# A fused attention and ELU layer on one core: a new written-out order, Strassen for two more groups, DMA transposes for two more blocks

## The chip, the core and the metric

The kernel runs on one NeuronCore of a Trainium2 chip. The metric is the device time of one launch in microseconds (us). TensorE is called PE here, VectorE DVE, ScalarE ACT, GpSimd POOL and SyncE SP. Each has its own instruction stream and runs it in order; they meet at semaphores, and DMA transfers are issued from the SP, ACT and POOL queues.

## What is computed

Decayed linear attention in blocks of 64 rows (4 batches, 8 heads, 768 rows, head size 64), then a dense layer of width 2048 with an ELU and a dense layer back to 512:

```python
for b in range(nb):                       # nb = 12 blocks of 64 rows
    intra = einsum('bhic,bhjc->bhij', qb, kb) * Dmask
    intra = einsum('bhij,bhjd->bhid', intra, vb)
    inter = einsum('bhid,bhde->bhie', qb * lam_pow, kv_state)
    out[:, :, sl] = intra + inter
    kv_state = lam_block * kv_state + einsum('bhsd,bhse->bhde', kb * rev_pow, vb)
x = out.transpose(0, 2, 1, 3).reshape(3072, 512)
h = x @ w_in                              # 512 -> 2048
g = where(h > 0, h, exp(min(h, 0)) - 1)
return g @ w_out                          # 2048 -> 512
```

## The kernel before

The work is cut into 24 steps `s`; a step is one block of 64 rows of two batches, so 128 rows of `x` (even steps belong to batches 0 and 1, odd steps to 2 and 3). What the title of the change calls a block is a step here. Two steps make a group of 256 rows, 12 groups in all. All products are in fp16.

**Attention of a step.** `load` brings `kn`, `qn`, `vn` in with casting DMAs on POOL's queue, in two halves of 64 partitions with rows of 64 numbers; the queries of steps 0 to 5 come as rows of eight (`eights`, one transfer with 2 KB rows), and step 0's keys and queries come uncast on SP's and ACT's queues into `kraw0`, `qraw0`. `visit(so, us, ss, sx)` issues PE work for up to four steps at once: `mm_S` scores of `ss` (into psum tile `Z`), `mm_U` the state update of `us`, `mm_I` and `mm_O` the output of `so`, and the transposes of `sx` (`mm_T`, or for early steps the 128-wide form at lines 398 and 403). Beside it stand, by letter of the order: `C` (`att_C`) copies transposes out of psum, `P` multiplies scores with the mask, `N` adds the new state, `X` (`att_X`) copies the output into `xt`, `V` (`decay_v`) forms `vd` = `vn` times the decay, which `mm_U` reads, `Q` (`decay_q`) forms `qs` and `D` (`decay_s`) forms `sd`. From step `NT` = 10 on the transposes come from `dma_T`, two DMA transposes on SP's queue into `TD`, with two buffers.

**Dense layers of a group.** `mm1_h` (H, line 428) makes 512 columns of `h` in psum tile `psH` (two buffers), 8 such units a group. `mm1_e` or `elu` apply exp and relu on ACT (lines 438, 440, 472, 474), and DVE combines them (`g`, lines 445 and 475). For groups 0, 1 and 2 (steps 0 to 5) the second layer is plain: `mm2` (M, line 495), four pieces of 4 products of 512 columns a step, and `mm2_o` (Z) stores. From group 3 on it is one level of Strassen: `g_sum` (s, line 533) and `w_sum` (B, line 521) form sums on DVE, `part` (p, line 551) runs 7 pieces of 8 products of 256 columns a group, `keep`, `add` and `c2` move and add the parts (lines 581, 585, 589), `store` writes.

**The order.** `tc.manual_schedule()` keeps each engine's stream as the program issues it. Up to step 8 the order is the string `start`, one word per call (`A...2` is a visit that transposes step 2, `V2` is `decay_v(2)`); `later_loads` (word R) and the lines before it fix POOL's load order. From group 3 on, a loop over groups and units interleaves the units with visits, parts and sums. POOL runs `decay_q` and `decay_s` of late steps between its load issues. Each transfer from POOL uses one of eight completion semaphores in turn, so an issue waits for the landing of the eighth transfer before it.

```python
    load("v", 0)
    load_step(1)
    load_wi(0)
    load_step(2)
    load_wi(1)
```

Of the kernel before, what the change touches and what calls it, by code (L numbers as in the profile page):

```python
# [16 lines left out]
def kernel(  # L17
# [41 lines left out]

    NB = 12  # L60

    NT = 10

    NQ = 6
    kn, qn, vn = {}, {}, {}

    def eights(b, c):

        return q[b : b + 2, :, c * L : (c + 1) * L, :].rearrange("r h (p g) d -> (r h) p (g d)", g=8)

    def load(which, s):
        b, c = where(s)
        src, keep, tag = {"k": (k, kn, "kn"), "q": (q, qn, "qn"), "v": (v, vn, "vn")}[which]
        keep[s] = inp.tile([128, H, D], FP16, tag=tag, bufs=NB, name=f"{tag}{s}")
        if which == "q" and s < NQ:
            nc.gpsimd.dma_start(out=keep[s][:].rearrange("p h d -> p (h d)"), in_=eights(b, c))
            return
        for r in range(2):
            nc.gpsimd.dma_start(  # L79
                out=keep[s][half(r)],  # L80
                in_=src[b + r, :, c * L : (c + 1) * L, :].rearrange("h p d -> p h d"),
            )

    def load_step(s):
        load("k", s)
        load("q", s)
        load("v", s)
# [9 lines left out]
    def load_wi(i, halves=range(2)):  # L97

        for c in halves:
            ins = nc.gpsimd.dma_start(  # L100
                out=wi[i][half(c)],
                in_=moe_w_in[c * DM // 2 : (c + 1) * DM // 2, i * WB : (i + 1) * WB].rearrange(
                    "(g p) f -> p g f", p=64
                ),
            )
            if (i, c) == (2, 1):

                ins.wait_op(crossed, 1, "sem-ge")

    def load_wo(i):  # L110
        nc.gpsimd.dma_start(
            out=wo[i][:],
            in_=moe_w_out[i * WB : (i + 1) * WB, :].rearrange("(g p) f -> p g f", p=128),
        )

# [5 lines left out]
    for which, src in (("k", k), ("q", q)):  # L121
        raw0[which] = inp.tile([128, H, D], FP32, name=f"{which}raw0")
        if which == "q":
            nc.scalar.dma_start(out=raw0[which][:].rearrange("p h d -> p (h d)"), in_=eights(0, 0))
            continue
        for r in range(2):
            nc.sync.dma_start(
                out=raw0[which][half(r)], in_=src[r, :, 0:L, :].rearrange("h p d -> p h d")
            )
    load("v", 0)  # L130
    load_step(1)
    load_wi(0)
    load_step(2)
    load_wi(1)
    load_step(3)
    load_wi(2, [0])

# [95 lines left out]
    def att_C(s):  # L233
        if s >= NT:
            return
        T = asb.tile([128, 2, NHP, 2, L], FP16, tag="T", bufs=4, name=f"T{s}")
        psT = st[s].pop("psT")
        if s < NQ:
            nc.vector.tensor_copy(T[:, 0].rearrange("p j r t -> p (j r t)"), psT[0])
            nc.scalar.copy(  # L240
                out=T[:, 1].rearrange("p j r (t g) -> p (j r t) g", g=8),
                in_=psT[1].rearrange("p (g x) -> p x g", g=8),
            )
        else:
            nc.vector.tensor_copy(
                T[:].rearrange("p i j r t -> p r (i j) t"),
                psT.rearrange("p r (x t) -> p r x t", t=L),
            )
        st[s]["T"] = T

# [11 lines left out]
    def att_X(s, eng):  # L262
# [5 lines left out]
        if eng is nc.scalar:  # L268
            nc.scalar.copy(out=to, in_=O)
        else:  # L270
            eng.tensor_copy(to, O)
# [23 lines left out]
    def visit(so, us, ss, sx, begin=False):  # L295
# [23 lines left out]
        if sx is not None and sx < NQ:  # L319
            psT = st[sx]["psT"] = (psT[0][:, : NHP * L].bitcast(FP16), psT[1][:])  # L320
# [71 lines left out]
        if sx is not None and sx < NQ:  # L392
# [3 lines left out]
            for g in range(8):  # L396
                for x in range(2):
                    nc.tensor.matmul(
                        psT[1][half(x), g * 64 : (g + 1) * 64], lhsT=qn[sx][:, g, :], rhs=of[x],
                        start=True, stop=True, skip_group_check=True,  # L400
                    )
            for j in range(NHP):
# [32 lines left out]
    def mm1_e(grp, c0, nc_, n0):  # L435
# [4 lines left out]
        nc.scalar.activation(r[:], psH[:], AF.Relu)  # L440
# [22 lines left out]
    def elu(grp, u):  # L463

        psH, nb, T, name = unit[grp, 0, 2, u]
        if grp == 3 or grp == 4 and u < 6:
            mm1_e(grp, 0, 2, u)
            mm1_g(grp, 0, 2, u, NF2)
            return

        r = msb.tile([128, nb, T], FP32, tag="r", bufs=4, name=f"r{name}")
        nc.scalar.activation(r[:], psH[:], AF.Relu, scale=-1.0)  # L472
        e = msb.tile([128, nb, T], FP32, tag="e", bufs=4, name=f"e{name}")
        nc.scalar.activation(e[:], r[:], AF.Exp, scale=-1.0)  # L474
# [6 lines left out]
    nacc = [0]  # L481
# [8 lines left out]
    def mm2(s, n0):  # L490
        if n0 == 0:
            acc[s] = M[nacc[0] % 2][:]
            nacc[0] += 1
# [6 lines left out]
    def mm2_o(s):  # L500
        o = msb.tile([128, DM], FP32, tag="o", bufs=4, name=f"o{s}")
        nc.scalar.copy(out=o[:], in_=acc.pop(s))
# [56 lines left out]
    def part(grp, i):  # L559
        d = res.setdefault(grp, dict(A=M[0], B=M[1]))  # L560
        lo, hi = slice(0, HD), slice(HD, DM)
# [6 lines left out]
    def store(s, o, cols, queues=(nc.sync, nc.sync)):  # L568
        for r in range(2):
            queues[r].dma_start(out=rows(s, r)[:, cols], in_=o[half(r), cols])  # L570
# [7 lines left out]
    def keep(grp, tag, src, bufs=2):  # L578

        t = res[grp][tag] = msb.tile([128, *src.shape[1:]], FP32, tag=tag, bufs=bufs, name=f"{tag}_{grp}")  # L580
        nc.scalar.copy(out=t[:], in_=src)
# [5 lines left out]
    def c2(grp, queues=(nc.sync, nc.sync)):  # L587
# [5 lines left out]
        store(2 * grp + 1, d[1], slice(0, DM), queues)  # L593
# [12 lines left out]
    def later_loads():  # L606
        load_wi(2, [1])
        load_wo(0)
        load_wi(3)
        load_wo(1)  # L610
        load_wo(2)
        load("k", 4)
        load("q", 4)
        load_wo(3)
        load("v", 4)
        load_step(5)
        load_step(6)
        load_step(7)
        load_step(8)
        load("k", 9)  # L620
        load("q", 9)
        load("k", 10)
        load("q", 10)
        load("v", 9)
        load("k", 11)
        load("q", 11)
        load("v", 10)

    start = (
# [14 lines left out]
    )  # L646
    steps = {
        "I": lambda s: visit(s, None, None, None, True), "C": att_C, "P": att_P, "X": lambda s: att_X(s, nc.scalar),
        "Y": lambda s: att_X(s, nc.vector), "N": att_N, "D": lambda s: decay_s(s, eng=nc.vector), "L": load_step,
        "V": lambda s: decay_v(s, nc.vector if s < 99 else nc.gpsimd),  # L650
        "Q": lambda s: decay_q(s, nc.vector if s < 10 else nc.gpsimd),
        "H": mm1_h, "E": mm1_e, "G": mm1_g, "M": mm2, "Z": mm2_o, "K": consts, "B": w_sum, "T": dma_T,
    }
    for word in start.split():
        if word[0] == "A":
            visit(*(int(x) if x else None for x in word[1:].split(".")))
        elif word[0] == "R":
            later_loads()
        elif word[0] == "F":
            cast0(word[1])  # L660
        else:
            steps[word[0]](*(int(x) for x in word[1:].split(".") if x))

    lo, hi = slice(0, HD), slice(HD, DM)

    five = [(3, 2), (3, 4), (3, 6), (4, 0)]
    nload = 12
    for grp in range(3, NG):  # L670
        old, new = grp - 2, grp - 1
        for u in range(8):
            mm1_h(grp, 0, 2, u, NF2)
            s = 2 * grp + 2 + u // 4
            if s < NS and u % 4 == 0:

                if nload < NS:
                    load("k", nload)
                    load("q", nload)
                if nload <= NS:  # L680
                    load("v", nload - 1)
                    nload += 1
            if s < NS and u % 4 == 1:
                if s not in (10, 12):
                    decay_q(s + 1, nc.vector if s < 10 else nc.gpsimd)
# [125 lines left out]
```

## Time and profile before

| what | value |
|---|---|
| time, median of 3 runs | 206.41 us (205.39, 206.41, 207.72) |
| span of the profiled execution, first to last instruction | 204.2 us |
| its distance from the median of the runs | 2.2 us |
| PE, DVE, ACT, POOL busy | 189.6, 168.7, 146.5, 123.4 us |
| mean granted TensorE clock | 0.996 |

The profile has one execution; its own time is its span and what lies before the first and after the last instruction, which the page does not list by itself, so the 2.2 us between span and median stand for it. Busy times count an instruction from start to end, and neighbours on an engine overlap a little, so DVE's and ACT's busy time is more than the time that they occupy.

### The profile page before, as it was taken

To read this page: it belongs to the slowest core of one execution; us is meant where nothing else is said; L and a number is where in the kernel's file an instruction comes from. 1 tells how busy PE (TensorE), PEld (TensorE's weight loads), DVE (VectorE), ACT (ScalarE), POOL (GpSimd) and SP (SyncE) were. 2 spreads that over 40 slices of the span, in tenths; PEclk is the share of its full clock that TensorE was granted. 3 is DMA by queue.
4 is the path that set the end of the run, shared out by engine and by line. 5 is a ranking of instruction groups with operands and counts; after the bars stand their busy time and mean duration, and the time that the engine had idled before them with its cause. 6 is when DMAs were issued, how large, how long until landed. Compare 5 with 4: busy or idle time off the path is not lost.

```text
span 204.2 us, 7590 instructions
## 1 busy us (share of the span) xinstructions
PE 189.6 (93%) x3216; PEld 156.6 (77%) x3216; DVE 168.7 (83%) x279; ACT 146.5 (72%) x283; POOL 123.4 (60%) x174
## 2 busy tenths in 40 slices
PE   0679899999999999999999989999999999999991
PEld 0457777647777777888888878888888888888881
DVE  4776996489989998999989999989979866758672
ACT  5626987635774879999878677788688788876820
POOL 8977832598998959997709999999222200020000
PEclk9999999999999999999999999999999999999998
DMA  6999999999999999999999999999915404004043
GB/s 102 157 171 171 152 206 196 180 124 156 117 148 150 173 108 172 153 134 78 74 163 109 206 105 86 185 111 105 169 27 69 94 0 108 0 6 100 3 103 103
DMA packets 94194, 24.36 MB, mean 119 GB/s; under 512 B 86160, under 2 KB 91152, under 8 KB 94160
## 3 DMA queue, kind: packets, MB, share of 16 engines
q0 software_dynamic: 73744, 13.64, 94.7%
q1 hardware_dynamic: 19968, 9.77, 26.9%
q10 hardware_dynamic: 448, 0.46, 1.0%
q8 instruction: 25, 0.41, 0.9%
q14 instruction: 9, 0.07, 0.1%
HBM read 27.27 MB, written 6.29 MB: 164 GB/s over the span
## 4 chain that ended last, share of the span: by engine, by line
PE 85%; DVE 4%; DMA 3%; POOL 3%; issue 2%; ACT 1%; POOLq 0%; DVEq 0%
PE psH L428 40%; PE psM L551 23%; PE psM L495 10%; DMA wi<-in_moe_w_in_dram 3%; PE psO_None L328 2%; POOL vn L79 1%; PE psZ L352 1%; PE psO_None L337 1%; PE psHB L551 1%; PE psHA L551 1%; DVE s L533 1%; PE psZ L344 1%; DVE g L475 1%; POOL kn L79 1%; PE psO L359 1%
## 5 line engine op out<-in xcount | busy, mean ns | idle before, releaser
L428 PE MATMUL psH<-xt,wi 128*128 128x256 f16 (+1 forms) x896 | 100.1, 261 | 1.9 <-ACT e L438 0.6
L428 PEld LDWEIGHTS <-wi 128*128 128x128 f16 x896 | 78.2, 100 | 13.3 <-issue 2.1
L475 DVE SCALAR_TENSOR_TENSOR g<-e,psH 128x512 f16<-128x512 f32 x58 | 39.6, 683 | 14.3 <-ACT e L474 13.8
L472 ACT ACTIVATE r<-psH 128x512 f32<-128x512 f32 x58 | 34.7, 598 | 18.3 <-PE psH L428 18.2
L474 ACT ACTIVATE e<-r 128x512 f32<-128x512 f32 x58 | 36.5, 630 | 1.8
L79 POOL DMA_DIRECT2D kn<-in_k_dram x46 | 32.2, 720 | 9.2 <-DMA wo<-in_moe_w_out_dram 5.1
L79 POOL DMA_DIRECT2D vn<-in_v_dram x48 | 34.1, 741 | 2.0 <-DMA wi<-in_moe_w_in_dram 1.1
L438 ACT ACTIVATE e<-psH 128x512 f32<-128x512 f32 x38 | 22.8, 601 | 14.7 <-PE psH L428 14.4
L551 PEld LDWEIGHTS <-s 128*128 128x128 f16 x288 | 28.1, 98 | 3.3
L445 DVE SCALAR_TENSOR_TENSOR g<-e,r 128x512 f16<-128x512 f32 x38 | 25.7, 685 | 4.1 <-ACT r L440 4.0
L220 POOL TENSOR_TENSOR qs<-TD,powi 128x512 f16<-128x512 f16 x11 | 13.9, 1264 | 19.3 <-PE psO_None L328 13.1
L79 POOL DMA_DIRECT2D qn<-in_q_dram x36 | 25.3, 735 | 0.0
L551 PE MATMUL psM<-wt,s 128*128 128x256 f16 x192 | 24.9, 273 | 0.0
L495 PE MATMUL psM<-wo,g 128*128 128x512 f16 x96 | 24.0, 379 | 0.0
L440 ACT ACTIVATE r<-psH 128x512 f16<-128x512 f32 x38 | 22.9, 602 | 0.0
L551 PEld LDWEIGHTS <-g 128*128 128x128 f16 x216 | 20.6, 98 | 2.6
L193 DVE TENSOR_TENSOR vd<-vn,rev 128x512 f16<-128x512 f16 x22 | 17.2, 783 | 1.8 <-DMA vn<-in_v_dram 1.7
L228 DVE TENSOR_TENSOR P<-psZ,mask 128x512 f16<-128x512 f32 x24 | 16.4, 684 | 2.0 <-PE psZ L344 1.1
L551 PE MATMUL psM<-wo,g 128*128 128x256 f16 x136 | 17.6, 272 | 0.0
L495 PEld LDWEIGHTS <-g 128*128 128x128 f16 x96 | 8.7, 98 | 7.0
L570 POOL DMA_DIRECT2D out_dram<-o x2 | 1.1, 574 | 21.1 <-DVE o L585 21.1
L533 DVE TENSOR_TENSOR s<-g 128x1024 f16<-128x1024 f16 x18 | 13.8, 764 | 0.0
(85 smaller groups left out, 228.7 us busy)
## 6 DMA issues: line engine op xcount, KB each, us to landing
out_dram<-o SPq DMA_DIRECT2D x43, 128.0 KB, 3.3
vn<-in_v_dram POOLq DMA_DIRECT2D x48, 64.0 KB, 5.0
kn<-in_k_dram POOLq DMA_DIRECT2D x46, 64.0 KB, 4.3
qn<-in_q_dram POOLq DMA_DIRECT2D x36, 64.0 KB, 4.5
wi<-in_moe_w_in_dram POOLq DMA_DIRECT2D x8, 256.0 KB, 8.9
wo<-in_moe_w_out_dram POOLq DMA_DIRECT2D x4, 512.0 KB, 12.6
qn<-in_q_dram POOLq DMA_DIRECT2D x5, 128.0 KB, 5.3
kraw<-in_k_dram SPq DMA_DIRECT2D x2, 128.0 KB, 4.7
```

Source lines behind the costliest of these rows:

```text
L79: nc.gpsimd.dma_start(out=keep[s][half(r)], in_=src[b + r, :, c * L : (c + 1) * L, :].rearrange("h p d -> p h d"),)
L193: eng.tensor_tensor(out=st[s]["vd"][:], in0=vn[s][:], in1=rev[:].unsqueeze(2).broadcast_to([128, H, D]), op=ALU.mult,)
L228: nc.vector.tensor_tensor(out=d["P"][:].rearrange("p y j t -> p y (j t)"), in0=psS, in1=mask[:].rearrange("p y j t -> p y (j t)"), op=ALU. ...
L428: nc.tensor.matmul(psH[:, i, :], lhsT=wi[n // 4][:, kk, (n % 4) * 128 : (n % 4 + 1) * 128], rhs=xt[grp][:, kk, c0 * 128 : c0 * 128 + T], s ...
L438: nc.scalar.activation(e[:], psH[:], AF.Exp)
L440: nc.scalar.activation(r[:], psH[:], AF.Relu)
L445: nc.vector.scalar_tensor_tensor(out=place(grp, c0, nc_, n0, nb, step), in0=e[:], scalar=-1.0, in1=r[:], op0=ALU.add, op1=ALU.min,)
L472: nc.scalar.activation(r[:], psH[:], AF.Relu, scale=-1.0)
L474: nc.scalar.activation(e[:], r[:], AF.Exp, scale=-1.0)
L475: nc.vector.scalar_tensor_tensor(out=place(grp, 0, 2, u, 2, NF2), in0=e[:], scalar=-1.0, in1=psH[:], op0=ALU.add, op1=ALU.max,)
L495: nc.tensor.matmul(acc[s], lhsT=g_of(s, n), rhs=wo[n // 4][:, n % 4, :], start=(n == 0), stop=(n == NFT - 1),)
L551: nc.tensor.matmul(to, lhsT=lhsT, rhs=rhs, start=start and n == 0, stop=stop and n == NF2 - 1, skip_group_check=True,)
```

## The change

1. **One order.** The string `plan` holds every call of the kernel, loads and stores included; the loop over groups, `later_loads` and the closing sequence are gone. On each engine nearly everything changes place. New options in the words pick the engine: `V2.1` is `decay_v(2)` on POOL, `C1.1` copies the keys' transposes on ACT, `E0.0.1.0.1` does the relu on DVE.
2. **Strassen for groups 1 and 2** (steps 2 to 5). `mm2` stays for group 0 alone. This adds 8 `g_sum`, 6 adds and 6 `keep` copies.
3. **DMA transposes from step 8 on** (`NT` = 8): four more on SP's queue, and the 128 PE transposes of steps 8 and 9 with DVE's two copies go.
4. **Step 0's keys as rows of eight** (`NK` = 1): one transfer with 2 KB rows in place of two with 256 B rows. They are transposed by plain products with `ident` and transposed back by `rows_of_k` (4 products) and `copy_k` for the state update.
5. **Unread products** (`unread`, word Y): 36 products of `ident` with itself into `psU`, whose results nothing reads: 12 ahead of the first transposes, 2 behind them, 20 behind `rows_of_k`.
6. **Work moved.** POOL gets `vd` of 13 steps (2, 4, 6, 9, 12 to 15, 17 to 21), `qs` of 8, 10, 13 and `sd` of 4, 8, 9, 10, and gives up `qs16`, `sd16`, `sd21`: 36 elementwise instructions in place of 19. ACT copies the transposes of steps 6 and 7 and those of the keys of steps 1 to 3; DVE takes those of the queries of steps 0, 2 and 5, four `c45`, two `p2` and two `u` copies, `xt` of step 12 and four relus. DVE issues 285 instructions in place of 279. The wait on `crossed` ahead of the sixth piece of `w_in` is gone.

```diff
+    plan = (
+        "K1 Y4 Y4 Fk lv0 Y4 Fq A...0 C0.0.1 Y2 R0 r0.0 Y2 Y2 Y4 Y2 Y2 lk1 Y2 Y2 Y4 Y2 lk2 lq1 "
+        "w0.0 lv1 w0.1 lq2 w1.0 lv2 lv3 lq3 V0 A.0.. lk3 K0 w1.1 w2.0 A..0. N0 P0 V2.1 A...1 lk6 "
+        "V1 C1.1 A.1.. A0... X0 w2.1 lq4 A..1. A...2 D2 lq5 P1 lk4 A1... H0.0.1.0 N1 D3 X1 w3.1 "
+        "lv4 H0.1.1.0 w3.0 C2.1.1 lk5 Q2 I2 E0.0.1.0.1 E0.1.1.0 A.2.2. P2 A2... X2 A...3 C3.1 "
...
+        "y2 G1.0.2.12 X4 E0.0.2.14 G1.1.1.0 lk7 G1.0.2.14 E1.1.1.8 H0.0.2.12 H2.0.1.12 M0.4 C6.1 "
+        "D5 M1.4 lq7 E0.0.2.12 N4 Q5 E2.0.1.12 H2.0.1.4 E2.0.1.4 M1.8 B1.0 H2.0.1.8 G1.1.1.8 y3 "
+        "M0.8 lv6 D6 P5 B1.1 E2.0.1.8 lq8 lk8 lv8 V5 s1.1 A5.5.6.7 X5 B2.0 H2.0.1.0 H2.1.1.0 "
...
+    )
...
-    NT = 10
+    NT = 8
     NQ = 6
+    NK = 1
...
+    def unread(n):
+        for _ in range(n):
+            nc.tensor.matmul(
+                psU[:, 0, :128], lhsT=ident[:], rhs=ident[:],
+                start=True, stop=True, skip_group_check=True,
+            )
+
+    def rows_of_k(s):
+
+        bank = ps.tile([128, 512], FP32, tag="h", bufs=2, name=f"psK{s}")
+        to = st[s]["psK"] = bank[:, : NHP * L].bitcast(FP16)
+        for j in range(NHP):
+            nc.tensor.matmul(
+                to[:, j * 128 : (j + 1) * 128], lhsT=st[s]["T"][:, 0, j].rearrange("p r t -> p (r t)"),
+                rhs=ident[:], is_transpose=True, start=True, stop=True, skip_group_check=True,
+            )
...
-            if (i, c) == (2, 1):
-
-                ins.wait_op(crossed, 1, "sem-ge")
...
-    for word in start.split():
+    for word in plan.split():
         if word[0] == "A":
             visit(*(int(x) if x else None for x in word[1:].split(".")))
-        elif word[0] == "R":
-            later_loads()
+        elif word[0] in loads:
+            loads[word[0]](word[1:])
...
-    for grp in range(3, NG):
-        old, new = grp - 2, grp - 1
-        for u in range(8):
-            mm1_h(grp, 0, 2, u, NF2)
...
```

In the words, small `l` is a load (`lk1`), `w` and `y` pieces of `w_in` and `w_out`, small `h`, `e`, `g` the units of groups 3 to 11, `k`, `a`, `c`, `o` the copies, adds and stores behind the parts `p`.

More of the change, by code (lines that the diff above doesn't have):

```diff
@@ L95, with load_wi @@
     crossed = tc.alloc_semaphore("crossed")
[L97 to L105, printed above, removed]
-            if (i, c) == (2, 1):
-                ins.wait_op(crossed, 1, "sem-ge")
+    def load_wi(i, c):
+        nc.gpsimd.dma_start(
+            out=wi[i][half(c)],
+            in_=moe_w_in[c * DM // 2 : (c + 1) * DM // 2, i * WB : (i + 1) * WB].rearrange(
+                "(g p) f -> p g f", p=64
+            ),
+        )
     def load_wo(i):
@@ L122 @@
         raw0[which] = inp.tile([128, H, D], FP32, name=f"{which}raw0")
[L123 to L136, printed above, removed]
+        eng = nc.scalar if which == "q" else nc.sync
+        eng.dma_start(out=raw0[which][:].rearrange("p h d -> p (h d)"), in_=eights(0, 0, src))
     ident = cst.tile([128, 128], FP16, name="ident")
@@ L592, in c2 @@
         )
-        store(2 * grp + 1, d[1], slice(0, DM), queues)
     def consts(i):
@@ L631, with sums @@
-    start = (
[14 rows of a table removed]
-    )
-    steps = {
[L648 to L652, printed above, removed]
+    def sums(grp, i):
+        d = res[grp]
+        if i == 0:
+            add(grp, 0, hi, d["A"][:, hi], "p35")
+        if i == 1:
+            add(grp, 0, lo, d["A"][:, hi], "p2")
+        if i == 2:
+            add(grp, 0, hi, d["B"][:, hi], "u2")
+        if i == 3:
+            add(grp, 0, lo, M[1][:, lo], "u1")
@@ new lines, in by @@
+    def by(eng):
+        return nc.gpsimd if eng else nc.vector
+    steps = {
+        "I": lambda s: visit(s, None, None, None, True), "C": att_C, "P": att_P,
+        "X": lambda s, e=0: att_X(s, nc.vector if e else nc.scalar), "N": att_N, "D": lambda s, e=0: decay_s(s, eng=by(e)),
+        "d": lambda s, a, b: decay_s(s, range(a, b)), "V": lambda s, e=0: decay_v(s, by(e)),
+        "Q": lambda s, e=0: decay_q(s, by(e)), "H": mm1_h, "E": mm1_e, "G": mm1_g, "M": mm2, "Z": mm2_o,
+        "K": consts, "B": w_sum, "T": dma_T, "R": rows_of_k, "r": copy_k, "Y": unread, "h": lambda g, u: mm1_h(g, 0, 2, u, NF2), "e": elu_e,
+        "g": elu_g, "s": g_sum, "p": part_of, "a": sums, "c": c2, "o": store,
```

274 lines of the change are left out of this document (97 added, 177 removed), and 59 rows, old and new, of tables (plan, start).

## The prediction

> **What bounds the kernel now.** First the page: busy times, slices and the chain that ended last.
>
> ```profile
> PE 189.6 (93%) x3216; PEld 156.6 (77%) x3216; DVE 168.7 (83%) x279; ACT 146.5 (72%) x283; POOL 123.4 (60%) x174
> PE   0679899999999999999999989999999999999991
> ...
> PEclk9999999999999999999999999999999999999998
> DMA  6999999999999999999999999999915404004043
> ...
> PE 85%; DVE 4%; DMA 3%; POOL 3%; issue 2%; ACT 1%; POOLq 0%; DVEq 0%
> ```
>
> PE is the chain for 85% of the span and full in nearly every slice from the sixth on; DMA is full for three quarters of the span. So a gain must come out of PE's own work or out of its few holes, and a new order may run into DMA. Next the chain in order of time, for what PE's pieces cost and where it waits.
>
> ```profile
> 7.01 6.18 DMA wi<-in_moe_w_in_dram
> 13.24 1.89 PE psH L428 x16
> ...
> 16.24 1.71 PE psH L428 x16
> ...
> 22.60 0.49 ACT T L240
> ...
> 29.11 0.89 PE psH L428 x16
> ...
> 46.80 0.29 PE psO L359 x32
> ...
> 49.85 0.86 PE psM L495 x4
> ...
> 81.76 0.87 PE psM L551 x8
> ...
> 93.79 0.98 PE psH L428 x8
> ...
> 108.49 0.98 PE psH L428 x8
> ...
> 124.03 0.98 PE psH L428 x8
> ...
> 138.73 0.98 PE psH L428 x8
> ...
> 200.22 0.42 DVE o L585
> ```
>
> Columns: start, duration, what. Dense work begins at 13.24 us, when the first `w_in` pieces have landed, and ends near 200.2, before the last add and store. A unit of `h` (16 products of 128 columns, or 8 of 256) costs 0.87 to 0.89 us. Three things stand out. The first two units cost 1.89 and 1.71 us, twice the later 0.89, while PEclk reads full. A group takes 138.73 - 124.03 = 14.70 us, and so does the one from 93.79 to 108.49; the one between takes 15.54. And at 22.60 ACT is in the chain.
>
> **The change, part by part.** *Strassen.* A step of `mm2` is four pieces of 0.86 us, so a group costs 8 x 0.86 = 6.9; seven Strassen pieces of 0.87 cost 6.1. Two groups save 1.6 us of PE, which is the bound, so all of it counts: -1.6.
>
> *DMA transposes of steps 8 and 9.* The 32 PE transposes of a step took 0.29 in the chain: -0.6. DVE loses two copies as well. The cover is SP's queue: `TD8` goes behind the four stores of steps 1 and 0.
>
> ```profile
> 66.10 1.11 SPq L504 DMA_DIRECT2D out_dram<-o  x2
> ...
> 82.32 1.19 SPq L256 DMA_TRANSPOSE TD<-kn  x1
> ```
>
> ```profile
> TD<-qn SPq DMA_TRANSPOSE x14, 5.3
> ```
>
> From step 0's last product of M it is a copy on ACT (0.5), two stores (1.1), one transpose's issue (1.2) and the second's landing (5.3), 8.1 us, until the scores of step 8 can be formed in visit 7; PE has nine units and pieces and visit 6 in between, some 8.6 us. I take nothing; it costs 0.9 for each unit that the cover comes out shorter.
>
> *The slow group.* In the timeline of that group:
>
> ```profile
> 113.26 1.59 POOL L220 TENSOR_TENSOR qs<-TD,powi 128x512 f16<-128x512 f16 x1
> ...
> 114.90 1.51 DVE L533 TENSOR_TENSOR s<-s,g 128x1024 f16<-128x1024 f16 x1
> ...
> 120.08 1.58 DVE L193 TENSOR_TENSOR vd<-vn,rev 128x512 f16<-128x512 f16 x1
> ...
> 121.00 1.55 POOL L211 TENSOR_TENSOR sd<-st,lamL 128x512 f32<-128x512 f16 x1
> ```
>
> and the groups that these belong to:
>
> ```profile
> L533 DVE TENSOR_TENSOR s<-g 128x1024 f16<-128x1024 f16 x18 | 13.8, 764 | 0.0
> ...
> L220 POOL TENSOR_TENSOR qs<-TD,powi 128x512 f16<-128x512 f16 x11 | 13.9, 1264 | 19.3 <-PE psO_None L328 13.1 <-PE psM L551 6.1
> ...
> L211 POOL TENSOR_TENSOR sd<-st,lamL 128x512 f32<-128x512 f16 x8 | 9.4, 1174 | 2.3 <-DVE st L281 2.3
> ```
>
> Where a POOL elementwise instruction and a DVE one with two SBUF operands run side by side, both stretch, DVE's to 1.5 us against a mean of 0.76. After the change nine `vd` and `qs13` leave DVE in the later steps and two `sd` and one `qs` come, so DVE has room there: -0.8 (15.54 - 14.70), between 0 and -0.8, since POOL then has 36 such instructions to collide with instead of 19. The Trainium skill speaks against this part: "GPSIMD Engine Reference", section Engine selection, gives elementwise work to VectorE because GpSimd is about half as fast with two inputs. The rows agree (1.26 us here); its consequence is the slow rival below.
>
> *The start.* Here most is unknown, since the traffic is reordered. The rows that price it:
>
> ```profile
> 12.16 0.61 POOL L100 DMA_DIRECT2D wi<-in_moe_w_in_dram  x1 [0.57 <-DMA wi<-in_moe_w_in_dram]
> 13.48 1.36 POOL L79 DMA_DIRECT2D kn<-in_k_dram  x2 [0.70 <-DMA wi<-in_moe_w_in_dram]
> ...
> 16.16 0.69 DVE L193 TENSOR_TENSOR vd<-vn,rev 128x512 f16<-128x512 f16 x1 [1.66 <-DMA vn<-in_v_dram]
> ...
> 28.33 0.78 POOL L111 DMA_DIRECT2D wo<-in_moe_w_out_dram  x1 [2.67 <-DMA wo<-in_moe_w_out_dram]
> ...
> 33.38 0.68 POOL L79 DMA_DIRECT2D kn<-in_k_dram  x1 [1.62 <-DMA wo<-in_moe_w_out_dram]
> ...
> 35.90 0.68 POOL L79 DMA_DIRECT2D kn<-in_k_dram  x1 [1.85 <-DMA wo<-in_moe_w_out_dram]
> ```
>
> POOL's waits tell landings: the two `w_in` pieces at 12.16 and 13.4, `w_out`'s first at 28.33, the others at 33.38 and 35.90, 2.5 apart. Between 13.4 and 16.16 the pairs `kn2`, `vn2` and the rows-of-eight `qn2` landed, so a pair takes 1.2 and rows of eight 0.5; a `w_in` piece takes 1.2. I lay these end to end in the new load order. `kn2` now stands ahead of the first `w_in` piece, which costs 1.2, and `kraw0` as rows of eight gives back some 0.7 (an estimate, 1.2 - 0.5): the second `w_in` piece lands at about 14.0. Then come `qn2`, a `w_in` piece and `vn2`, to 16.9. `vd2` is now POOL's, at 1.2, so the state update of step 2 waits until 18.1. PE is in order, so the output of step 2, the transposes of step 3 (whose inputs land at 19.8) and the next unit stand behind it. The first `w_out` piece has eight pairs, three rows of eight, five `w_in` pieces and itself ahead: 16.9 + 9.6 + 1.5 + 5.8 + 2.5 = 36.3 instead of 28.33, and M cannot begin before it; until then ACT, with two instructions of
>
> ```profile
> 30.04 0.60 ACT L438 ACTIVATE e<-psH 128x512 f32<-128x512 f32 x1 [0.51 <-PE psH L428]
> 30.54 0.59 ACT L440 ACTIVATE r<-psH 128x512 f16<-128x512 f32 x1
> ```
>
> that follow each other at 0.5, needs 1.0 for a unit that PE does in 0.87.
>
> Against that stands the clock. The unread products fill PE from the time that `ident` is ready, and the first two units could then cost 0.87 each: 1.89 + 1.71 - 1.74 = 1.9 saved, nothing if they stay slow. "TensorE: Matmul & The Clock Gate", Part 1, in the Trainium skill, says that PE starts at half rate and is released after some 3.4 us of sustained activity; the double cost until past 16.24 in the rows agrees, the granted clock does not show it. By that rule the saving would be the full 1.9.
>
> But the saving runs into the waits: at 18.1 both kernels have done the first two units and the scores of step 2. I walk on through the new order with these prices: H1.0.1.0 ends at 21.2, seven units by 28.3, M0.0 from 36.2. At 50.1 us the new order has done 22 units and 8 pieces of M, 30 in all, and visits 4 and 5. The old one has its 30th (18 units, 12 pieces) behind it at 49.85, with visit 5 still to come. A visit costs (14.70 - 15 x 0.87) / 2 = 0.8, with transposes 1.1, which makes 50.95. The start brings -0.8. The bounds: if loads do not hold PE up, the clock's 1.9 and the two waits behind `vd2` and `kn3` (1.2 and 0.5) come back, -4.4; if each of the some 25 loads lands a tenth of a microsecond later than laid out, 2.5 later, +1.7.
>
> *DVE between visits 5 and 8.* Strassen for group 1 comes just as DVE forms the sums of weights. From B1.0 to G2.1.1.12 the order gives DVE 39 instructions.
>
> ```profile
> 99.99 0.68 DVE L475 SCALAR_TENSOR_TENSOR g<-e,psH 128x512 f16<-128x512 f32 x1
> 100.58 0.68 DVE L533 TENSOR_TENSOR s<-s,g 128x1024 f16<-128x1024 f16 x1
> ```
>
> They follow each other at 0.59, so 39 make 22.6, three of them short adds (0.42 at the end of the chain). PE's share of the same stretch, up to p2.4, which reads the last `g` of group 2, is 19 units and pieces and three visits, 19.2. B1.0 may start about 2 us ahead of PE, when the third `w_out` piece lands. 22.6 - 19.2 - 2.0 = 1.4 of PE waiting; with no wait if DVE gets further ahead, 0, with two stretched instructions 3.0. I take +1.0, nearer to the middle than to the end, since the visits and parts between lean on DVE only in places.
>
> *The rest at nothing.* The copies that change between ACT and DVE in the later steps lie under PE, which has 14.7 us a group where the new order gives DVE 10 to 13. The tail keeps its form (last part, last add, two stores); five stores now wait in SP's queue ahead of the last ones. Their cover is the nine parts behind the last unit, 7.8 us; without it, one issue of 0.6.
>
> **Sum**, against the execution's own span: 204.2 - 1.6 - 0.6 - 0.8 - 0.8 + 1.0 = 201.4. The median of the runs lies 2.2 above the span, so 203.6 us.
>
> **Rivals.** *A, the early loads do not hold PE.* [...] Against it: DMA is full from the second slice on. Start at -4.4, DVE's wait 0: 204.2 - 1.6 - 0.6 - 0.8 - 4.4 = 196.8, or 199.0.
>
> *B, no change.* DVE's wait at 3.0 and no relief in the slow group: 204.2 - 1.6 - 0.6 - 0.8 + 3.0 = 204.2, or 206.4. For it speaks that DVE is full in the stretches beside visits 5 to 8 already; against it that DVE's waits there do not reach the chain today.
>
> *C, GpSimd becomes the bound, slower.* POOL's queue holds loads and elementwise work in one line, and the loads now come just before use.
>
> ```profile
> 58.89 1.51 POOL L79 DMA_DIRECT2D vn<-in_v_dram  x2
> ...
> 109.19 1.39 POOL L79 DMA_DIRECT2D kn<-in_k_dram  x2
> ```
>
> From about 48 us, when the last `w_out` piece has let it go, POOL has 19 pairs and 10 elementwise instructions until `qs12`, which visit 12 needs at about 93 by PE's pace: with 1.4 and 1.2, done at 87; with the stretched 1.5 and 1.55, at 92.5. From that point it decides. 23 pairs and 19 instructions follow to `vd20`, needed at 150: 55 us at the low prices, 64 at the high, so 156.5, 6.5 late: 201.4 + 6.5 = 207.9, or 210.1. For it: contention in the rows above at 1.5 to 1.6 for both engines. Against it: the mean of POOL's instructions is 1.2, and 6 us of slack. That products in the new order miss their purpose (the clock stays at half rate) is inside the bound of the start: +1.9 at most, 203.3, or 205.5.
>
> **Chances.** The forecast 0.45, A 0.17, B 0.2, C 0.18. The forecast's own range is 201 to 205.5; the range that leaves out a fifth is 199.0 to 209.0, from A's value to short of C's. Within 1% is about 2 us, near what a measurement of this kernel tells from none. Faster by over 1% (below 204.3): A and most of the forecast, 0.55. Within 1%: B and a part of the forecast, 0.23. Slower: C and the tail of B, 0.22.
>
> **What would show it.** Right: the first unit at about 14 us at 0.9; `vd2` on POOL ending near 18 with PE waiting for it; the first M piece near 36; groups of 14.7 us throughout from visit 9 on; 64 products of 512 columns gone and 112 of 256 come. Wrong: a first M before 30 (A); PE waiting for DVE by over 2 us between 50 and 70 (B); PE waiting for POOL's `vd` or `qs` after 90 (C); units at 1.7 us after 16 us (the clock).

## The result and the profile after

The changed kernel takes 222.15 us (median of 4 runs, 219.24 to 223.19), the kernel before 206.15 (4 runs of the same series): ratio 1.069, 95% interval 1.060 to 1.079. Two of the changed kernel's four runs (223.09 and 223.19) were slow ones; the ratio is of the fast ones alone. By the ratio it is slower by some 14 us where 3 us of gain were forecast. The profiled execution took 219.24 us, its span is 217.5, so 13.3 us more span than before are to be explained.

The page of the changed kernel:

```profile
PE 191.9 (88%) x3252; PEld 162.7 (75%) x3252; DVE 182.3 (84%) x286; ACT 142.6 (66%) x274; POOL 143.2 (66%) x191
...
PE   2847979989969989948999999979989999999991
...
PEclk9999999999997999999999999999999999999999
...
PE 52%; DMA 16%; DVE 16%; POOL 6%; issue 4%; ACT 2%; SPq 1%; POOLq 0%; DVEq 0%
```

PE's own work grew by 2.3 us, its idle time by 11.0 (217.5 - 191.9 against 204.2 - 189.6). DVE has 7 instructions more (286 by the page, where the list of the change has 285) and 13.6 us more busy time, and the chain, 85% PE before, now runs through DVE and DMA for 32%. Busy time by stage; the two numbers at the head are the window's ends and its length, then come PE, PEld, DVE, ACT and POOL with their instructions, the granted clock, the DMA share and GB/s. Before, and then after:

```profile
54.00:65.00 11.00, 11.00 (x287) 7.96 (x285) 10.40 (x18) 6.92 (x14) 10.46 (x16) 1.00 1.67 149
...
73.00:100.00 27.00, 27.00 (x472) 22.70 (x473) 25.47 (x43) 24.65 (x53) 23.41 (x33) 1.00 1.86 120
...
135.00:165.00 30.00, 30.00 (x504) 26.29 (x503) 25.81 (x42) 24.00 (x44) 12.61 (x15) 1.00 0.86 88
```

```profile
54.00:65.00 11.00, 9.09 (x212) 7.92 (x210) 7.48 (x13) 6.52 (x14) 10.01 (x14) 0.96 1.85 147
65.00:73.00 8.00, 8.00 (x120) 6.58 (x118) 7.83 (x12) 3.89 (x8) 7.00 (x9) 0.84 1.68 137
73.00:100.00 27.00, 22.38 (x336) 18.34 (x330) 26.88 (x33) 18.14 (x38) 25.62 (x32) 1.00 1.37 101
...
135.00:165.00 30.00, 27.68 (x424) 24.01 (x422) 26.21 (x38) 21.91 (x39) 25.37 (x30) 1.00 1.10 120
```

Between 73 and 100 us PE has no idle time before and 4.6 us after. DVE is full, and gets 33 instructions done where the kernel before did 43. Its chain there, after (start, duration, what):

```profile
72.86 0.19 PE psO_None L400 x8
73.05 0.69 DVE st L353
...
74.34 1.46 DVE s L619
...
77.11 1.45 DVE g L521
...
82.14 1.51 DVE vd L232
...
89.09 1.46 DVE s L619
90.58 1.41 DVE s L619
91.99 2.35 DVE g L521
94.34 1.27 DVE s L619
...
99.89 0.32 PE psZ L424 x16
```

For 27 us the chain does not touch PE. Seven of its instructions last 1.27 to 2.35 us in place of the slot of 0.6, 6.7 us in all. All seven read both operands from SBUF; those with one in psum (`P`, `st`, `o`) keep 0.6. The longest has two products of GpSimd beside it, as the timeline shows:

```profile
91.91 2.43 DVE L521 SCALAR_TENSOR_TENSOR g<-e,r 128x512 f16<-128x512 f32 x1
...
92.68 1.10 POOL L232 TENSOR_TENSOR vd<-vn,rev 128x512 f16<-128x512 f16 x1
93.69 1.67 POOL L259 TENSOR_TENSOR qs<-TD,powi 128x512 f16<-128x512 f16 x1
```

Two smaller losses lie ahead of it. PE waits 1.9 us for step 8's transposes, and works at a granted clock of 0.84 behind that hole (a part and two units, at 1.82 and 2.28 us in the chain, in place of 0.87 and 1.75):

```profile
53.24 0.59 ACT o L274
53.83 0.92 ACT T L274
...
56.97 6.89 DMA TD<-qn
...
64.83 1.82 PE psM L637 x8
66.65 2.28 PE psH L501 x16
```

And the start is late (timeline of PE):

```profile
53.04 1.06 PE L501 MATMUL psH<-xt,wi 128*128 128x128 f16 x16
53.93 1.91 PE L637 MATMUL psM<-wo,g 128*128 128x256 f16 x16
```

At 53.93 the new order has its 22 units, 8 pieces of M and visits 4 and 5 behind it, for which the prediction had 50.1, against 50.95 by its count of the kernel before. The first two units end near 17.7 us here and near 17.9 in the kernel before, so the loss is made behind them: from 18 to 54 us PE waits for 3.9 us here (1.0 for `w_out`, the rest in pieces of 0.3 to 0.7 for `P`, ACT, `vd2` and `w_in`) and for 1.3 before.

### The profile page after: what moved, and what is told of

Same layout as the page of the kernel before. It is cut to its first block, busy times and chain, and to the rows that moved or that the text cites. A ratio compares the mean times of both kernels' runs of the same rounds, so it can differ in the third digit from the quotient of the medians.

```text
span 217.5 us, 7668 instructions
## 1 busy us (share of the span) xinstructions
PE 191.9 (88%) x3252; PEld 162.7 (75%) x3252; DVE 182.3 (84%) x286; ACT 142.6 (66%) x274; POOL 143.2 (66%) x191
## 4 chain that ended last, share of the span: by engine, by line
PE 52%; DMA 16%; DVE 16%; POOL 6%; issue 4%; ACT 2%; SPq 1%; POOLq 0%; DVEq 0%
PE psH L501 24%; PE psM L637 20%; DMA wi<-in_moe_w_in_dram 9%; DVE g L521 4%; DMA wo<-in_moe_w_out_dram 4%; DVE s L619 4%; DMA TD<-qn 3%; DVE g L562 2%; PE psM L581 2%; PE psO_None L400 2%; POOL vn L135 1%; POOL kn L135 1%; DVE P L267 1%; PE psHB L637 1%; PE psHA L637 1%
## 5 line engine op out<-in xcount | busy, mean ns | idle before, releaser
L637 PEld LDWEIGHTS <-s 128*128 128x128 f16 x352 | 34.1, 98 | 5.6 <-DVE s L619 1.4
L521 DVE SCALAR_TENSOR_TENSOR g<-e,r 128x512 f16<-128x512 f32 x38 | 30.3, 820 | 1.5 <-ACT r L516 1.5
L637 PE MATMUL psM<-wt,s 128*128 128x256 f16 x240 | 31.1, 273 | 0.0
L637 PEld LDWEIGHTS <-g 128*128 128x128 f16 x264 | 25.8, 99 | 4.1 <-DVE g L521 0.8
L259 POOL TENSOR_TENSOR qs<-TD,powi 128x512 f16<-128x512 f16 x13 | 16.3, 1254 | 18.9 <-PE psO_None L400 13.6
L637 PE MATMUL psM<-wo,g 128*128 128x256 f16 x168 | 22.8, 280 | 0.2
L619 DVE TENSOR_TENSOR s<-g 128x1024 f16<-128x1024 f16 x22 | 18.6, 848 | 0.1
L274 ACT CAST xt<-psO_None 128x512 f16<-128x512 f32 x21 | 12.2, 583 | 8.4 <-PE psO_None L409 8.3
L250 POOL TENSOR_TENSOR sd<-st,lamL 128x512 f32<-128x512 f16 x10 | 11.5, 1147 | 7.5 <-DVE st L353 7.5
L232 POOL TENSOR_TENSOR vd<-vn,rev 128x512 f16<-128x512 f16 x13 | 16.1, 1245 | 0.1
L353 DVE TENSOR_TENSOR st<-psZ,sd 128x512 f16<-128x512 f32 x20 | 13.6, 680 | 0.2 <-PE psO_None L400 0.2
```

What stands on the lines that cost most here:

```text
L259: eng.tensor_tensor(out=st[s]["qs"][:], in0=st[s]["T"][:, 1], in1=powi[:].unsqueeze(2).broadcast_to([128, NHP, 2, L]), op=ALU.mult,)
L521: nc.vector.scalar_tensor_tensor(out=place(grp, c0, nc_, n0, nb, step), in0=e[:], scalar=-1.0, in1=r[:], op0=ALU.add, op1=ALU.min,)
L619: nc.vector.tensor_tensor(out=gs[grp, i][:], in0=a, in1=b, op=ALU.add if i == 1 else ALU.subtract)
L637: nc.tensor.matmul(to, lhsT=lhsT, rhs=rhs, start=start and n == 0, stop=stop and n == NF2 - 1, skip_group_check=True,)
```

## Experiments

Theory 1: GpSimd's elementwise products stretch DVE's instructions with two SBUF operands, and DVE sets the time where they meet. Theory 2: DVE has too much to do, or in the wrong order, wherever GpSimd works. Theory 3: the late DMA transposes, with the clock that falls behind the hole. A fourth possibility is GpSimd's queue itself (the prediction's rival C).

**The forms by themselves** (`m1_forms`; a kernel of its own):

```diff
+    for d in (s_sum, g_er, lambda: vd(nc.vector, vo), g_ps, cp):
+        stage(d, None)        # eight on DVE alone
+        stage(d, pvd)         # eight on DVE, six vd on GpSimd
+    stage(s_sum, pm)          # GpSimd's memset beside it
```

> Nothing of the layer is computed; DVE and GpSimd run the layer's elementwise forms in stages, each form first by itself and then beside GpSimd's product of `vd` (eight on DVE, six on GpSimd). Theory 1, stretching beside GpSimd: the forms with two operands in SBUF (`s`, `g` from `e` and `r`, `vd`) take 0.6 to 0.7 us alone and 1.2 to 2.0 beside GpSimd, and the forms with an operand in psum (`g` from `psH`, the copy) stay below 0.75 beside it. Theory 2, the amount and the order of DVE's work: the stretched rows of the trace are waits for something else, and every form stays below 0.8 in both kinds of stage. The stage of `s` beside GpSimd's memset tells whether it is GpSimd's reading that counts, and the stages beside GpSimd's load issues whether issues stretch DVE too.

The timeline: six `vd` on GpSimd alone; `s` alone, then beside them; `g` from `psH` alone, then beside them; `s` beside memsets; `s` beside load issues.

```profile
4.25 6.64 POOL L82 TENSOR_TENSOR po<-p,p 128x512 f16<-128x512 f16 x6
...
11.03 5.76 DVE L73 TENSOR_TENSOR so<-x,y 128x1024 f16<-128x1024 f16 x8
...
16.83 10.24 DVE L73 TENSOR_TENSOR so<-x,y 128x1024 f16<-128x1024 f16 x8
...
17.52 8.28 POOL L82 TENSOR_TENSOR po<-p,p 128x512 f16<-128x512 f16 x6
...
59.09 5.72 DVE L79 SCALAR_TENSOR_TENSOR go<-e,P 128x512 f16<-128x512 f32 x8
...
64.84 5.74 DVE L79 SCALAR_TENSOR_TENSOR go<-e,P 128x512 f16<-128x512 f32 x8
...
84.68 5.75 DVE L73 TENSOR_TENSOR so<-x,y 128x1024 f16<-128x1024 f16 x8
...
90.47 11.57 DVE L73 TENSOR_TENSOR so<-x,y 128x1024 f16<-128x1024 f16 x16
```

Theory 1 holds: one product on GpSimd costs DVE (10.24 - 5.75) / 6 = 0.75 us, and itself grows by 0.27. `g` from `e` and `r` and `vd` gave 10.25 and 10.24 as well. With an operand in psum, beside memsets or beside issues there is nothing. So a product of 0.72 us that is moved from DVE to GpSimd takes 0.75 from DVE, as long as DVE has such instructions beside it. "SBUF — State Buffer" in the Trainium skill, section Who interferes with whom, states this rule: a DVE instruction with two SBUF inputs contends with a GpSimd instruction that reads SBUF, not with one that only writes. The stages agree; the same page's full exclusion they do not bear out, since 5.75 + 6.64 would make 12.4 us in a row and the stage took 10.2.

**GpSimd's products left out** (`a_without_pool_work`):

```diff
+        if eng is nc.gpsimd:
+            st[s]["vd"] = vn[s]     # and so for qs and sd
+            return
```

> The changed kernel without GpSimd's 36 elementwise instructions: `vd`, `qs` and `sd` of those steps are not formed, and the products read `vn`, `TD` and the old state in their place. Its loads and its order stay. Theory 1: seven stretched DVE instructions in the chain between 73 and 100 us last 6.7 us more than their slots of 0.6, and some 2 us more lie between 135 and 165, so the span falls from 217.5 to about 208 (206 to 210), and DVE's busy time from 182 to about 170. Theory 2: DVE has the same instructions in the same order, and the span stays above 214.

231.75 us in its one run, slower still, by another way: DVE's busy time fell to 166.3, as theory 1 has it, but GpSimd's loads ran ahead (its last keys were issued from 111.55 us on, in the changed kernel from 152.51) and `TD` came late four times (waits of PE; us in total, times, longest):

```profile
PE psZ L433 <- DMA TD<-qn: 8.9, 4, 3.6
```

The kernel changed two things at once and decides nothing about the time.

**GpSimd as busy, but only writing** (`a_pool_writes_only`):

```diff
+    def writes(to, read):
+        nc.gpsimd.tensor_copy(to[:, 0:1], read)
+        for _ in range(2):
+            nc.gpsimd.memset(to[:, 1:], 0.0)
```

> The changed kernel with each of GpSimd's 36 products replaced by a copy of one column of its input and two memsets over its output tile, so `vd`, `qs` and `sd` of those steps hold zeros. The waits, the place in GpSimd's queue and the time that it is busy (0.2 + 2 x 0.57 us against 1.2) stay, so the loads keep their pace, which they did not in the kernel without GpSimd's work; but GpSimd reads almost nothing. Theory 1, GpSimd's reading stretches DVE: the seven stretched instructions of the chain between 73 and 100 us return to 0.7, and a few behind 135, so 209 to 213 us, DVE busy about 168. Rival, GpSimd's occupancy or lateness delays the chain: as slow as the changed kernel, 217 to 223. Theory 2, amount and order of DVE's work: above 216, with DVE still in the chain.

210.28 us, ratio to before 1.025 (1.017 to 1.033) against the changed kernel's 1.069. Its page, and its busy times in the dense stretch:

```profile
PE 191.7 (92%) x3252; PEld 164.9 (79%) x3252; DVE 166.8 (80%) x286; ACT 142.8 (68%) x274; POOL 144.0 (69%) x263
```

```profile
73.00:100.00 27.00, 27.00 (x477) 23.81 (x477) 24.00 (x41) 23.25 (x50) 25.08 (x44) 1.00 1.43 115
```

With the same instructions on DVE, the same order and as busy a GpSimd, PE has no idle time there and DVE 15.5 us less busy time. Theory 2 and the occupancy of GpSimd fall for this part: the reads cost 1.069 - 1.025 = 4.4% of 206, some 9 us, give or take 2.5 by the two intervals.

**Where they cost** (`a_writes_steps_8_13`): the same for ten products alone (`if eng is nc.gpsimd and 8 <= s <= 13`).

> The changed kernel with ten of GpSimd's 36 products as writes only, those of steps 8 to 13 (`sd8`, `qs8`, `vd9`, `sd10`, `sd9`, `qs10`, `vd13`, `vd12`, `qs12`, `qs13`, at 61 to 106 us in its trace); these hold zeros. Theory 1, with the place: the reads beside DVE's dense stretch of 73 to 100 us make most of the loss, 6 to 8 us of the 10 to 12 that all 36 made, so 213 to 216.5, and the waits between 135 and 165 stay. Rival, the loss is spread evenly over the 36: 10 / 36 of 11 us, 218 to 220.

213.82 us, ratio 1.042 (1.035 to 1.050): ten of the 36 make (1.069 - 1.042) x 206 = 5.5 of the 9 us, again give or take 2.5; an even share of ten in 36 would be 2.5. PE is full from 73 to 100, the waits behind 135 stay. The place counts, as expected.

**Back on DVE** (`a_products_back_on_dve`): `V2.1` becomes `V2` and so on.

> The changed kernel with the 20 products that it gave to GpSimd (13 `vd`, 3 `qs`, 4 `sd`) back on DVE at the same places of the order; GpSimd keeps 16. The stage with `s` beside six products on GpSimd took DVE 10.24 us against 5.75, so a product on GpSimd costs DVE (10.24 - 5.75) / 6 = 0.75, and one on DVE 5.76 / 8 = 0.72. Theory 1: the move gave DVE nothing, so undoing it costs nothing, 215 to 221 us, DVE busy near 180. Rival, the move did relieve DVE and the loss is elsewhere: the 20 come back at 0.6 to 0.7 on a DVE that sets the time for at least half of them, 224 to 232.

223.94 us, ratio 1.093 (1.085 to 1.101): slower than theory 1's bound, and at the lower edge of the rival's range. DVE has 20 instructions more and is busy for 184.2 us against 182.3, so the offload had relieved it of 1.9 us in all. The time is not clean, by the edit itself: `vd2` now stands on DVE ahead of `vd1`, and DVE waits there for `vn2`.

```profile
17.58 1.29 DVE L232 TENSOR_TENSOR vd<-vn,rev 128x512 f16<-128x512 f16 x2 [4.79 <-DMA vn<-in_v_dram]
```

So `P` of step 1 began at 19.83 us instead of 13.63, and visit 7 formed its scores 7 us later too. The busy time supports theory 1; the run's time decides nothing.

**More work for GpSimd in the kernel before** (`b_16_pool_products`, `b_16_pool_memsets`):

```diff
+        if 5 <= s <= 12:
+            extra(s)        # two products (or copies with memsets) on GpSimd
```

> The kernel before with 16 more products on GpSimd, two behind each new state of steps 5 to 12, each from the state into a tile that nothing reads, 128x512 like `sd`. DVE, PE and ACT have the instructions and the order of before. Theory 1: they stretch some 16 DVE instructions by 0.6 to 0.9 us, 10 to 14 us in all, of which DVE's idle time between 50 and 100 (2.5 us) and what waits elsewhere take a part: slower by 4 to 10 us. Theory 2: no change beyond 1 us, 205.5 to 207.5.

> The kernel before with 16 additions at the places of the 16 products of the run that took 216.1 us, each a copy of one column and two memsets of 128x511, so that GpSimd is as busy and its loads as late, without reading more than a column. Theory 1: within 1.5 us of the kernel before. Rival, the lateness of the loads behind the additions: 213 to 217, like the products.

216.11 us (one run) and 213.02 (ratio 1.038, 1.029 to 1.048). Theory 1's expectation of the second fell: most of this loss is lateness, not reading. A wait of the memset kernel:

```profile
PE psO_None L338 <- POOL qs L220: 4.2, 1, 4.2
```

Here `qs` comes too late behind the additions, the mechanism of rival C, which the kernel before has little slack for. The reading shows in DVE's busy time, on the pages of the kernel with products and of the one with memsets:

```profile
PE 193.2 (90%) x3216; PEld 157.9 (74%) x3216; DVE 181.6 (85%) x279; ACT 146.7 (68%) x283; POOL 145.4 (68%) x190
```

```profile
PE 191.5 (91%) x3216; PEld 157.5 (75%) x3216; DVE 170.4 (81%) x279; ACT 146.9 (70%) x283; POOL 144.1 (69%) x222
```

181.6 - 170.4 makes 0.70 us for each of the 16, near the 0.75 of the stages.

**The kernel before with its own products as writes** (`b_own_products_as_writes`), the `writes` of above:

> The kernel before with its own 19 products on GpSimd as writes only (`qs` and `sd` of those steps hold zeros). Theory 1: the mean of DVE's `s` falls from 764 to 685 ns, DVE's busy time by 4 to 5 us, and the group that took 15.5 us takes 14.7: 0.5 to 1.5 us faster, which is all the relief that the prediction could have counted on. Rival, that group is slow for another reason: within 0.4 us of the kernel before.

205.23 us, ratio 0.9956 (0.9921 to 0.9992), 0.9 us faster, with 0.2 and 1.6 as the interval's ends. DVE is busy for 164.2 us, and the scores of the same two visits (PE), in the kernel before and then here, show the slow group gone, 123.36 - 107.81 = 15.55 against 122.74 - 108.04 = 14.70:

```profile
107.81 0.30 PE L352 MATMUL psZ<-TD 64*64 64x64 f16 x16
...
123.36 0.30 PE L352 MATMUL psZ<-TD 64*64 64x64 f16 x16
```

```profile
108.04 0.30 PE L363 MATMUL psZ<-TD 64*64 64x64 f16 x16
...
122.74 0.30 PE L363 MATMUL psZ<-TD 64*64 64x64 f16 x16
```

**Transposes of steps 8 and 9 on PE**, in the changed kernel (`a_pe_transposes_8_9`) and where GpSimd only writes (`a_writes_pe_transposes_8_9`): `NT = 10`, `C8` and `C9` for `T8` and `T9`.

> The changed kernel with the transposes of steps 8 and 9 on PE and their copies on DVE, as before the change. Theory 3, the late DMA transposes: PE's wait of 1.9 us at 64 and the two units and pieces after it at a lowered clock, 2.6 us more, are on the path, and the span falls by 3 to 4.5 us to 213 to 214.5. Theories 1 and 2: DVE sets the time between 73 and 100, gets two copies more, and at most the 2.7 us that it idles between 55 and 65 come back, so 215.5 to 217.5.

> The kernel whose GpSimd writes only (zeros for 36 `vd`, `qs`, `sd`), with the transposes of steps 8 and 9 back on PE. In the former's chain the wait for `TD8` and the pieces after it at a lowered clock are all on PE's path: 64.5 to 73.0 us hold seven pieces of 0.87 and a visit, 1.8 us more than these need, and PE waited 2.5 us before. Theory 3, the late DMA transpose costs its full length once DVE does not set the time: 2.5 + 1.8 - 0.6 = 3.7 us less than the kernel that writes only, 206 to 207.5. Rival, something else is late behind it, as with the full kernel, where this edit brought nothing: above 209.

221.38 (one run) and 209.66 us. The first lies above all that was expected, among the changed kernel's own runs (219.24 to 223.19): there the wait is hidden, as DVE still fills the stretch behind it (26.92 of 27 us from 73 to 100). In the other one it brought 0.6 us, which its interval (1.015 to 1.027) does not tell from nothing. Two things took the gain away in its trace, and both stand ahead of visit 6, where the edit begins: step 2's `P` came 1.2 us later (20.60 against 19.45), and PE stood in visit 5, in the middle of step 7's transposes, for 1.4 us, for which the profile names no releaser (`issue`):

```profile
PE psO L445 <- issue: 1.4, 1, 1.4
```

**Step 8 earlier in the queues** (`a_writes_early_t8`):

```diff
-  ... G1.1.1.8 y3 ... E2.0.1.8 lq8 lk8 lv8 V5 ... A5.5.6.7 X5 ... N6 T8 p1.6
+  ... G1.1.1.8 lq8 lk8 y3 ... E2.0.1.8 lv8 V5 ... A5.5.6.7 T8 X5 ... N6 p1.6
```

> The kernel whose GpSimd writes only, with `q8` and `k8` loaded ahead of the last `w_out` piece and `T8` issued right after visit 5, ahead of the four stores of steps 1 and 0. Theory 3, PE's wait of 2.5 us at 62 and the 1.8 us at a lowered clock behind it come from where the loads and the transposes stand in the queues: both go, 206 to 207.5 (the same edit by PE transposes brought 0.6 us, since visit 6 then waited 1.4 us for the late `kn8` and the start came out 1.2 later). Rival, it is crowding of the DMA engines and not the place in a queue: 209 to 211.

208.18 us, ratio 1.0115 (1.008 to 1.015): 1.35%, 2.8 us, for the place in the queues, give or take 1.7. It lies above the expected 207.5, and its start was late like the last one's (`P` of step 2 at 20.73). In both of these executions the granted clock was 0.50 from 15 to 20 us, against 1.00 in the changed kernel's, though the order of the start is the same in all three: this lateness belongs to the execution. From 54 us on PE has no idle time left:

```profile
54.00:65.00 11.00, 11.00 (x235) 9.31 (x233) 9.35 (x17) 7.94 (x16) 8.45 (x16) 1.00 1.79 158
65.00:73.00 8.00, 8.00 (x133) 7.01 (x131) 7.79 (x15) 4.89 (x10) 7.88 (x13) 1.00 1.56 111
```

**The start** in three kernels: unread products added to the kernel before (`U12` ahead of `A...0`, `U22` behind `C0`), the old start in the kernel that only writes, and, in the kernel with `T8` early, `w_out` earlier (`y0` ahead of `lq4`, `M0.0` and `M1.0` around `A..4.`).

> The kernel before with the 34 unread products at the start alone: 12 ahead of the first transposes and 22 behind step 0's copies. Theory of the prediction: they bring the two first units from 1.89 and 1.71 us to about 0.9 each, but PE then runs into waits, so between 1.9 and 0 us faster, and I take 0.5 to 1.2. Rival: they delay the first scores by their own time, 34 x 0.06 to 0.12 us, on a path that DMA does not cover, and it is slower by 0.5 to 2.

> The kernel whose GpSimd writes only, with the start of the kernel before: step 0's keys as rows of 64 numbers in two transfers, no unread products, no products that transpose them back; the order of the rest stays. Theory 4, the added products at the start stand ahead of the first scores: `P` of step 0 began at 9.24 us before and at 11.37 after the change, so the first unit comes 1 to 2 us earlier and the end too, 208.3 to 209.5. Theory of the prediction, the unread products bring the clock and pay: the first units double, and the end is later by 0 to 1.9, 210.3 to 212.

> The kernel that writes only, with `T8` early, and besides with the first `w_out` piece loaded ahead of `q4` and the first two pieces of M ahead of visits 4 to 5, behind the 11th unit. In the former PE waited for nothing from 54 us on, so what is left to the kernel before (1.2%, and 2.2 us of PE work saved) lies in the start: PE 12.1 of 14 us busy from 40 to 54, 1.8 us of it one wait for a `w_out` piece. Theory 5, PE has only units there, each with two instructions of ACT, and the late `w_out` pieces leave it nothing else: 0.8 to 2 us faster than the kernel with `T8` early, 206 to 207.4. Rival, DMA is full and what one load gains another loses: 207.8 to 209.5.

The first took 207.70 us, 1.0135 (1.006 to 1.021): slower, as the rival had it, but by some 2.8 us instead of 0.5 to 2, and not in the way that it named. Its first units:

```profile
14.45 1.89 PE L428 MATMUL psH<-xt,wi 128*128 128x128 f16 x16
...
17.20 1.06 PE L428 MATMUL psH<-xt,wi 128*128 128x128 f16 x16
```

The first one still has the double cost, behind holes of 0.6 and 0.9 us that came after the unread products, and begins 1.2 us later than before. That is made good: a piece of M begins at 54.93 us, where the kernel before begins it at 55.16. What the trace loses, it loses in visit 8, in one hole for which the profile names no releaser:

```profile
69.77 0.32 PE L337 MATMUL psO_None<-P,vn 64*64 64x64 f16 x15 [2.26 <-issue]
```

So the cause of this kernel's loss stays open. The second kernel, 210.12 us, was as fast as its base of 210.28: neither theory was right, and within some 2 us, by the intervals, the unread products and the keys as rows of eight cost the new order nothing and bring it nothing. The third, 211.24 us, lost 3 us against the kernel with `T8` early, and its trace has new waits for what now lands later:

```profile
PE psONone L485 <- DMA qn<-in_q_dram: 2.0, 1, 2.0
...
PE psONone L490 <- DMA kn<-in_k_dram: 1.3, 1, 1.3
```

**Groups 1 and 2 without Strassen** (`a_plain_groups_1_2`): `M2.0` to `M5.12` and four `Z` for these groups' parts, sums, copies and adds.

> The changed kernel with groups 1 and 2 without Strassen: 16 pieces of 4 products of 512 columns at the places of the 14 parts, four copies on ACT, and without these groups' 8 `s` sums, 6 adds and 6 copies; GpSimd's products all stay. If DVE sets the time between 73 and 100 us (theory 1, or theory 2), it loses some 14 instructions of 0.6 to 1.4 us and PE gets 1.7 us more: faster than the changed kernel by 3 to 7 us, 214 to 218.5. Rival, DVE's count does not matter and the loss is in DMA or GpSimd's lateness: 221 to 225.

221.24 us, ratio 1.078 (1.071 to 1.084): no change within what the runs tell, as the rival had it, and theory 1's 214 to 218.5 was missed. DVE has 15 instructions fewer and 7.9 us less busy time, but S of step 8 still begins at 65 us behind late loads, with 3.7 us of PE's time lost from 54 to 73 (1.9 in the changed kernel), and DVE's stretched `s` and `g` of 89 to 100 us, group 3's, still are the chain there. So less work on DVE and no Strassen do not end the loss by themselves; that late loads have a share in it beside the stretching, this run leaves open.

**A try at a faster kernel** (`b_sd_on_act`): `decay_s(s + 1, eng=nc.vector if s < 10 else None)`.

> The kernel before with the eight `sd` of GpSimd (steps 14 to 21) as four instructions each on ACT; it is meant to beat both. Theory 1: GpSimd reads beside DVE 11 times instead of 19, the group that took 15.5 us instead of 14.7 loses up to 0.8, and ACT has room in a group of 14.7 us: 0 to 1 us faster. Rival, ACT waits in order for the new state and holds `r` and `e` of the next unit: 1 to 4 us slower.

207.68 us, ratio 1.010 (1.007 to 1.014). The rival was right; no version here that computes the layer beats the kernel before.

## Why the prediction was wrong

*The slow group, and what followed from it: the step that failed.* The prediction quoted the stretched pair (1.59 on POOL, 1.51 on DVE) and read it as a loss that the change would end, "between 0 and -0.8", with 36 products in place of 19. The 0.8 was real (0.9 in the kernel with its own products as writes). But the bound excluded a loss: with DVE full, every added product beside two-operand work takes back what its move gave (20 products moved, 1.9 us of DVE's busy time relieved). All 36 measured +9 us, 5.5 of them from steps 8 to 13; less the 0.9 that the 19 cost before, the term is about +8 in place of -0.8. The next step made it invisible: *DVE between visits 5 and 8* counted 39 instructions at the unstretched 0.59 and ended with group 2, at most two of them stretched, +3.0, and *the rest at nothing* gave DVE 10 to 13 us a group of 14.7. Inside the counted stretch PE waited for DVE not at all (its one wait from 50 to 73 us is the 1.9 for `TD8`), so the +1.0 measured 0; DVE set the time just behind it, from 73 to 100.

*DMA transposes.* The saving of 0.6 stood against a cover that was too short. The path was to take 8.1 us from step 0's last piece; it took 63.99 - 53.24 = 10.75: the landing was 6.9 us instead of 5.3, and the copy `o` was followed by `T7` on ACT. The cost of the place in the queues, once DVE no longer hides it, measured 2.8 us; the "0.9 for each unit" left out the clock behind the hole, as this execution had it.

*The start.* -0.8 forecast, +3.0 found, outside the bound of 1.7. `vd2` on POOL ended at 18.5 as forecast, M began at 38.55 instead of 36.2. The clock's saving came (two units in 1.96 us) but from 15.73 instead of 14.0, and it was the luck of this execution: in the kernel with `T8` early, with the same order at the start, the first two units lasted from 15.60 to 19.99, at a granted clock of 0.50. The 3.0 lie in the many small waits behind the second unit, where the prediction had reckoned with two. What makes them is not settled: within 2 us not the unread products and not the new form of the keys, and an earlier `w_out` only moved the waits to `qn` and `kn`, which fits the rival that DMA is full and one load gains what another loses.

*The sum with these:* 204.2 - 1.6 - 0.6 + 2.8 + 3.0 + 9 - 0.9 = 215.9, measured 217.5; 1.6 stay open. The 2.8 and the 9 are uncertain by 1.7 and 2.5, so the sum fits no closer than that; the Strassen term and the 0.6 are taken over here, no run measured them alone.

*The rivals.* A was wrong: M began later, not earlier. B named the right engine, with a third of the price, and a place too early: PE waits for DVE from 79 us on, and nowhere between 50 and 70. C had the right sign and engine for a wrong reason: GpSimd was not late, it was in DVE's way. Its lateness did appear, in the kernel before with 16 additions.

## What to carry to other kernels

Before work is moved from DVE to GpSimd, look at what DVE runs beside it: instructions with two SBUF operands lose as much (0.75 us a product here) as the move gives, those with an operand in psum nothing. A stretched row in a profile is a price for each further collision, so the bound of such a term is open on the side of loss. And when the suspected engine's work is taken out to test it, keep its time and its waits, or the queue behind it changes as well.

## What the runs showed that was not expected

A wait of 2 us can be paid twice: behind PE's hole at 62 us the granted clock read 0.84 over 65 to 73 us, and the three pieces there took 1.5 us more in all. It need not be: in `a_writes_steps_8_13` a hole of 2.2 us at the same place left the clock at 1.00 and the piece behind it at its usual length.

```profile
65.80 0.32 PE L438 MATMUL psZ<-TD 64*64 64x64 f16 x16 [2.20 <-DMA TD<-qn]
...
66.40 1.05 PE L651 MATMUL psM<-wo,g 128*128 128x256 f16 x8
```

"TensorE: Matmul & The Clock Gate", Part 1, in the Trainium skill has PE start at half rate until it has been busy for a while; the rows at 14.45 and at 64.83 us agree in kind. The page gives an idle window of some 3.4 us ahead of the half rate; here holes of 0.6 to 1.9 us went ahead of the double cost.
